# Sliding-window attention and squared-ReLU MLP: Q and K of batches 2 to 7 turned by transposing DMAs instead of 32x32 blocks on VectorE

## The chip, the cores and the metric

The kernel runs on one core of a Trainium2 chip. The metric is the device time of one execution in microseconds, as the median of several runs. TensorE (PE), VectorE (DVE), ScalarE (ACT), GpSimd (POOL) and SyncE (SP) run side by side, each with its own list of instructions, which it takes strictly in order; semaphores tie the lists together. SP and POOL issue DMAs, which 16 DMA engines carry out.

## The reference

```
# q, k, v: [8 batches, 8 heads, 576 tokens, 64], float32
scores = q @ k.T / sqrt(64)                    # within a head
mask   = |i - j| <= 32                         # a window of 65 tokens
attn   = softmax(where(mask, scores, -1e9))
x      = (attn @ v), heads side by side        # [4608 tokens, 512]
h      = x @ w_in                              # [512, 2048]
out    = (max(h, 0) ** 2) @ w_out              # [4608, 512]
```

## The kernel before, in words

**Attention.** A step is 64 queries of one batch with all 8 heads; there are 9 steps a batch, 72 in all. A step's scores (`scores`) are 8 matmuls into one PSUM bank, `sc`: the K tile `KT` (for two heads 128 rows, one half a head, with 32 zero columns at each end) against the zero-padded Q tile `QZ`, in which each head has its 64 rows and zeros in the other 64, so that two heads share one pass. ScalarE takes the exponential, VectorE multiplies by the mask (`pt`), `av` multiplies with V (and a column of ones, which yields the sum), VectorE divides (`rs`, `xr`). The result xr must be turned so that features lie on partitions (`xt`): in the first 26 steps by TensorE and a ScalarE copy, from then on by a transposing DMA issued by SP (`xturn`).

**MLP.** Tokens come in blocks of 512, nine blocks. `mm1` makes 512 columns of h from xt (`ht`), ScalarE the ReLU (`rt`), VectorE the square (`gt`); `mm2` accumulates 128 tokens of output in `outp`, ScalarE copies it to `oe`, SP stores it. Most matmuls are done in two halves of 64 columns (the mode "col" of `matmul`).

**How Q, K and V come in.** POOL issues all loads; they cast float32 to bfloat16. For batches 0 and 1, Q and K come token by token (`fine_load`: pieces of 128 tokens, the last of 64, eight runs of 64 elements a token), TensorE turns each piece (`fine_turn`), VectorE copies K into `KT`, ScalarE copies Q twice into `QZ` with a scale of 1 or 0 for each half, which also writes the zeros. For batches 2 to 7, `load_qk` brings four pairs of heads per tensor, with four tokens side by side (256 elements); `turn` lets VectorE turn 32x32 blocks into the stage `ST`, 16 instructions a batch; `spread` sends the stage to its rows in `KT` and `QZ` by 16 DMAs a batch, issued by SP. Every score of such a batch waits for all 16 (`qk_tags`). V goes to `VD`, and `copy_v` makes a second copy shifted by 64 tokens, `VX`, on VectorE.

**What sets the order.** Every operation is recorded (`Prog.rec`) with what it reads and writes, a planned duration and a key. `schedule` plays the whole program through with these durations and, on each engine, takes the ready operation with the smallest key; that order is then written out and is fixed. Keys count attention steps: step n has the key n - LEAD, block T of the MLP has keys about 8 T + TM, so LEAD says how far attention runs ahead. `FIRST` is the order of the first 39 loads, weights (`a` for w_in, `b` for w_out) among them; `UNITS` the order of block 0's mm1; `KQ` and `KVL` say how early the loads of later batches are issued, FK, FQ, VK0, VK1, VK, KM, MD, TM shift other keys. In gaps of the plan before 36 us the planner puts filler matmuls on zeros (`outp<-zz`), which keep TensorE running.

A transposing DMA as it stands in the kernel before, for xt:

```
e.dma_start(self.XT[:, n % RX].rearrange("p (j h) q -> p j (h q)", j=2), xr[:], transpose=True)
```

Of the kernel before, what the change touches and what calls it, by code (L numbers as in the profile page):

```python
# [31 lines left out]
UNITS = (  # L32
    (0, 128, 0), (128, 128, 4), (256, 256, 2), (128, 128, 12), (0, 128, 12), (128, 128, 8), (0, 128, 8),
    (256, 256, 14), (256, 256, 8), (0, 128, 4), (256, 256, 4), (128, 128, 0), (256, 256, 6), (256, 256, 10),
    (256, 256, 12), (256, 256, 0),
)
FIRST = (
# [6 lines left out]
)  # L44
WCH = ((0, 512), (512, 512), (1024, 1024))
# [213 lines left out]
class Gen:  # L259
# [5 lines left out]
    def alloc(self):  # L265
# [8 lines left out]
        self.RAW = {t: [sb(f"{t}raw{i}", [128, 9, 4, 64], BF16) for i in range(2)] for t in "qk"}  # L274
        self.ST = {t: sb(f"{t}st", [128, 2, 1152], BF16) for t in "qk"}
# [71 lines left out]
    def fine_load(self, b, t, x, key):  # L347
        t0, n = PIECES[x]
        s = (self.q if t == "q" else self.k)[b][:, t0:t0 + n, :].rearrange("h p d -> p h d")
        d = self.FR[t][b][0:n, x, :, :]  # L350
        self.p.rec("POOL", lambda e: e.dma_start(d, s), writes=[("fraw", b, t, x)], dma=(f"f{b}{t}{x}", 0), key=key,  # L351
                   dur=900 if n == 128 else 700, move=(n // 2, 14))

    def fine_turn(self, b, t, x, key):
# [13 lines left out]
        self.p.rec("PE", f, reads=[("fraw", b, t, x), "id"] + [("frz", b, t)] * (n < 128), writes=[tag], key=key, dur=4 * 58 if n == 128 else 4 * 30,  # L368
                   mode="col")
        src = ps[:, 0:4 * n].rearrange("p (j c) -> p j c", j=4)  # L370
        if t == "k":
            dst = self.KT[b][:, :, 32 + t0:32 + t0 + n]
            self.p.rec("DVE", lambda e: e.tensor_copy(dst, src), reads=[tag], writes=[("kf", b, x, 0)], key=key,
                       dur=430 if n == 128 else 300)
            return
# [5 lines left out]

    def load_qk(self, b, t, key):
        src = (self.q if t == "q" else self.k)[b]
        raw = self.RAW[t][b % 2]
        for g in range(4):
            s = src[2 * g:2 * g + 2, :, :].rearrange("h s d -> (h s) d").rearrange(
                "(m r j) d -> r m j d", r=32, j=4)
            self.p.rec("POOL", lambda e, g=g, s=s: e.dma_start(raw[32 * g:32 * g + 32], s),  # L388
                       writes=[("raw", t, b % 2, g)], dma=(f"{t}{b % 2}", b), key=key, dur=610, move=(18, 48))
# [20 lines left out]
    def copy_v(self, b, key, s0, s1):  # L410

        i, n = b % 2, s1 - s0
        rd = [("vd", i, s) for s in range(s0, s1)] + [("vdone", i)]
        for r in (0, 64):
            self.p.rec("DVE", lambda e, r=r: e.tensor_copy(self.VX[i][r:r + 64, s0 + r // 64:s1 + r // 64, :, :],  # L415
                                                           self.VD[i][r:r + 64, s0:s1, :, :]),
                       reads=rd, writes=[("vxc", i, r, s + r // 64) for s in range(s0, s1)], key=key,
                       dur=190 + 140 * n)
# [15 lines left out]
    def turn(self, b, t, dh, m0, n, key, gate):  # L434
        raw, st, i = self.RAW[t][b % 2], self.ST[t], b % 2
        src = bass.AP(raw, 256 * m0 + 32 * dh, [[2304, 128], [256, n], [64, 4], [1, 32]])
        dst = bass.AP(st, 1152 * dh + 128 * m0, [[2304, 128], [128, n], [1, 4], [4, 32]])
        self.p.rec("DVE", lambda e: e.transpose(dst, src),  # L438
                   reads=[("raw", t, i, g) for g in range(4)], writes=[("st", t, dh, m0)], key=key,
                   dur=40 + 320 * n, gate=gate)  # L440

    def spread(self, b, t, dh, key):
        st, i = self.ST[t], b % 2
        rd = [("st", t, dh, m0) for m0 in (0, 3, 5, 7)]
        old = [(t + "f", b - 2, x, hm) for x in range(5) for hm in range(2)] if b < 4 else []
        for s in range(2):
            for hm in range(2):
                r, g = 64 * hm + 32 * dh, 2 * s + hm
                dst = self.KT[i][r:r + 32, 2 * s:2 * s + 2, 32:32 + S_] if t == "k" else \
                    self.QZ[i][r:r + 32, 2 * s:2 * s + 2, hm, :]  # L450
                src = st[32 * g:32 * g + 32, dh, :].rearrange("p (h c) -> p h c", h=2)
                self.p.rec("SP", lambda e, a=dst, c=src: e.dma_start(a, c), reads=rd,  # L452
                           writes=[(t, i, s, r)], old=old, dma=(f"{t}t{i}", b), key=key, dur=600, move=(4, 45))


    def qk_tags(self, b, c):
        i = b % 2
        rows = [64 * dh + 32 * hm for dh in range(2) for hm in range(2)]
        rd = [("ktpad", i, 0), ("ktpad", i, 1)]
        if b < 2:  # L460
            for x in range((64 * c) // 128, min(575, 64 * c + 95) // 128 + 1):
                rd += [("kf", b, x, 0)]
            if c:
                rd += [("kf", b, (64 * c - 32) // 128, 0)]
            return rd + [("qf", b, c // 2, 0), ("qf", b, c // 2, 1)]
        return rd + [(t, i, s, r) for t in "qk" for s in range(2) for r in (0, 32, 64, 96)]

    def scores(self, n):
# [5 lines left out]
        def f(e):  # L474
            for j in range(4):
                for u in range(2):
# [7 lines left out]
                   reads=[("sc", n % 2)], writes=[("e", n % 2)], key=key, dur=560)  # L484
# [8 lines left out]
    def av(self, n):  # L493
# [7 lines left out]
        def f(e):  # L501
            for j in range(4):
                for u in range(2):
                    h = 4 * (j // 2) + j % 2 + 2 * u
                    mm = e.matmul(self.AVP[64 * u:64 * u + 64, VE * j:VE * j + VE], pt[:, 128 * j + 64 * u:128 * j + 64 * u + 64],  # L505
# [41 lines left out]
    def mm1(self, T, t0, n, d0, key, mode="col"):  # L547
# [7 lines left out]
        def f(e):  # L555
            for d in range(nd):
                for ft in range(4):
# [6 lines left out]
                   writes=[("ht", k % 2)], key=key, dur=864 if n > 128 else 900, pos=key, mode=mode)  # L564
        self.p.rec("ACT", lambda e: e.activation(rt[:], ht[:], ACTF.Relu), reads=[("ht", k % 2)],  # L565
                   writes=[("rt", k % 4)], key=key, dur=560)
        rr = rt[:].rearrange("p (d t) -> p d t", d=nd)
        us = range(t0 // 128, (t0 + n) // 128)
# [4 lines left out]
    def mm2(self, T, u, seg, key):  # L573
# [11 lines left out]
        if seg == 3:  # L585
            oe = self.OE[x % 3]
            self.p.rec("ACT", lambda e: e.activation(oe[:], op[:], ACTF.Copy), reads=[("outp", x % 2)],  # L587
                       writes=[("oe", x % 3)], old=[("mtmp", 0), ("mtmp", 1)] if x == 0 else [], key=key, dur=560)
# [109 lines left out]
```

## Time and profile before

| | |
|---|---|
| median of three runs | 319.61 us (317.69 to 320.3) |
| profiled execution | 320.36 us, span 318.7 us, mean granted clock 0.988 |
| busy: PE, DVE, ACT, POOL | 303.1, 211.0, 165.1, 89.0 us |
| DMA queue of POOL (q0) | 73136 packets, 18.36 MB |
| DMA queue of SP (q1) | 26112 packets, 19.54 MB |
| read from and written to HBM | 36.70 and 9.44 MB |

The span is the time from the first to the last instruction in the profiled execution, and its time is a little longer. In the profile, a row of digits is the busy share of 40 equal slices of the span, in tenths; "PE sc L478 <- DMA qz<-qst: 3.6, 3, 2.3" means that TensorE's matmuls at line 478, which write sc, waited for the DMA that writes qz from qst, 3.6 us in total, 3 times, 2.3 at most. Groups list busy time and mean duration in ns of one, then the idle time of the engine just before. SPq and POOLq are the queues of instructions that issue DMAs; "to landing" is the time from the issue to the semaphore that says the data is there.

### The profile page before, as it was taken

Reading aid. Unit: us, or ns where it says so; the run is one execution under the profiler, and the core shown is the slowest. Engines: PE = TensorE matmul, PEld = TensorE weight load, DVE = VectorE, ACT = ScalarE, POOL = GpSimd, SP = SyncE. Lnnn points to the kernel's source line nnn. Section 1 sums busy time; section 2 is a strip of 40 time slices with the busy share of each in tenths; the row PEclk is TensorE's granted clock in tenths of the full one; section 3 lists DMA queues with packets and bytes.
Section 4 is the critical chain, followed back from the end, with each engine's and each line's share of the span. In section 5 each row is a group of like instructions: output and inputs, shape, how many; then the busy total and the mean of one; then the engine's idle time right before and its main releaser. Section 6 shows DMA issues by size and latency. Waiting matters only on the chain.

```text
span 318.7 us, 9690 instructions
## 1 busy us (share of the span) xinstructions
PE 303.1 (95%) x4065; PEld 205.5 (64%) x4065; DVE 211.0 (66%) x529; ACT 165.1 (52%) x303; POOL 89.0 (28%) x128
## 2 busy tenths in 40 slices
PE   6798999998999999979989999999999999999995
PEld 2466887877977776757546666665665666556552
DVE  7475686958798888868848888898744444323300
ACT  2387767545835662446435645643654555435511
POOL 8999992432142324401504211100000000000000
PEclk9799999999999999999979999999999999999999
DMA  9999999999969948993999596635411211210021
GB/s 58 145 186 200 174 189 187 201 229 237 117 105 183 172 49 129 190 215 48 137 176 161 54 161 102 138 79 110 118 50 51 68 43 43 59 69 33 2 100 67
DMA packets 99291, 38.52 MB, mean 121 GB/s; under 512 B 72624, under 2 KB 93616, under 8 KB 99248
## 3 DMA queue, kind: packets, MB, share of 16 engines
q0 software_dynamic: 73136, 18.36, 60.2%
q1 hardware_dynamic: 26112, 19.54, 22.0%
q8 instruction: 32, 0.52, 0.7%
q14 instruction: 11, 0.09, 0.1%
HBM read 36.70 MB, written 9.44 MB: 145 GB/s over the span
## 4 chain that ended last, share of the span: by engine, by line
PE 77%; DMA 12%; POOL 4%; SPq 2%; DVE 2%; ACT 1%; issue 1%; ACTq 0%
PE outp L53 34%; PE ht L53 33%; DMA qz<-qst 5%; PE sc L478 4%; DMA w<-in_moe_w_in_dram 4%; DMA xt<-xr 3%; PE avp L505 2%; PE ht L51 2%; SPq L452 2%; POOL qfr L351 2%; POOL kfr L351 1%; POOL vd L397 1%; ACT rt L565 1%; PE sc L364 1%; PE trp L537 1%
## 5 line engine op out<-in xcount | busy, mean ns | idle before, releaser
L53 PE MATMUL outp<-w,gt 128*64 128x512 bf16 x1152 | 140.6, 379 | 0.0
L53 PE MATMUL ht<-xt,w 128*64 128x512 bf16 (+1 forms) x1280 | 134.6, 351 | 2.8 <-DMA xt<-xr 2.1
L565 ACT ACTIVATE rt<-ht 128x512 bf16<-128x512 f32 x144 | 85.9, 597 | 70.1 <-PE ht L53 57.7
L53 PEld LDWEIGHTS ht<-xt,w 128*64 128x64 bf16 x1280 | 85.0, 137 | 33.6 <-DMA xt<-xr 3.2
L569 DVE TENSOR_TENSOR gt<-rt 128x512 bf16<-128x512 bf16 x144 | 60.5, 422 | 54.3 <-ACT rt L565 52.8
L53 PEld LDWEIGHTS outp<-w,gt 128*64 128x64 bf16 x1152 | 67.4, 110 | 38.7
L483 ACT ACTIVATE e<-sc 128x512 bf16<-128x512 f32 x72 | 42.2, 595 | 20.1 <-PE sc L478 18.6
L397 POOL DMA_DIRECT2D vd<-in_v_dram x32 | 30.1, 972 | 56.0 <-PE avp L505 26.8
L587 ACT ACTIVATE oe<-outp 128x512 f32<-128x512 f32 x36 | 21.5, 598 | 44.2 <-PE outp L53 44.2
L438 DVE STREAM_TRANSPOSE kst<-kraw 128x256 bf16<-128x256 bf16 (+1 forms) x48 | 37.4, 821 | 0.3 <-DMA kraw<-in_k_dram 0.3
L438 DVE STREAM_TRANSPOSE qst<-qraw 128x256 bf16<-128x256 bf16 (+1 forms) x48 | 36.0, 824 | 0.0
L490 DVE TENSOR_TENSOR pt<-e,mask 128x512 bf16<-128x512 bf16 x72 | 29.8, 417 | 6.4 <-ACT e L483 5.4
L519 DVE TENSOR_TENSOR xr<-avp,rs 128x256 bf16<-128x256 f32 x72 | 30.5, 423 | 1.0
L478 PE MATMUL sc<-qz,kt 128*64 128x128 bf16 x576 | 27.0, 221 | 3.7 <-DMA qz<-qst 3.6
L478 PEld LDWEIGHTS sc<-qz,kt 128*64 128x64 bf16 x576 | 22.2, 111 | 12.1 <-issue 4.6
L517 DVE RECIPROCAL rs<-avp 128x4 f32<-128x4 f32 x72 | 13.1, 181 | 20.2 <-PE avp L505 19.6
L388 POOL DMA_DIRECT2D qraw<-in_q_dram x24 | 15.0, 668 | 23.4 <-DVE qst L438 15.8
L405 POOL DMA_DIRECT2D vx<-in_v_dram x16 | 10.2, 639 | 32.2 <-PE avp L505 27.6
L415 DVE COPY vx<-vd 64x528 bf16<-64x528 bf16 (+1 forms) x28 | 16.9, 608 | 3.1 <-DMA vd<-in_v_dram 2.6
L388 POOL DMA_DIRECT2D kraw<-in_k_dram x24 | 14.7, 653 | 7.9 <-DVE kst L438 7.1
L378 ACT ACTIVATE qz<-sc,half 128x512 bf16<-128x512 bf16 (+1 forms) x20 | 12.1, 647 | 9.1 <-PE sc L364 9.0
L505 PEld LDWEIGHTS avp<-vx,pt 128*64 128x64 bf16 x320 | 11.8, 112 | 4.8 <-issue 0.7
(40 smaller groups left out, 144.6 us busy)
## 6 DMA issues: line engine op xcount, KB each, us to landing
out_dram<-oe SPq DMA_DIRECT2D x36, 256.0 KB, 2.4
vd<-in_v_dram POOLq DMA_DIRECT2D x32, 128.0 KB, 5.7
kraw<-in_k_dram POOLq DMA_DIRECT2D x24, 144.0 KB, 11.2
qraw<-in_q_dram POOLq DMA_DIRECT2D x24, 144.0 KB, 10.0
kt<-kst SPq DMA_DIRECT2D x48, 72.0 KB, 3.4
qz<-qst SPq DMA_DIRECT2D x48, 72.0 KB, 3.5
w<-in_moe_w_out_dram POOLq DMA_DIRECT2D x4, 512.0 KB, 17.4
qfr<-in_q_dram POOLq DMA_DIRECT2D x8, 128.0 KB, 4.9
```

Source lines behind the costliest of these rows:

```text
L53: mm = e.matmul(out[r:r + 64], w[:, r:r + 64], x, start=start, stop=stop)
L388: self.p.rec("POOL", lambda e, g=g, s=s: e.dma_start(raw[32 * g:32 * g + 32], s), writes=[("raw", t, b % 2, g)], dma=(f"{t}{b % 2}", b), k ...
L397: self.p.rec("POOL", lambda e, s=s: e.dma_start(self.VD[i][:, s, :, 0:64], v[b, :, 32 + 128 * s:160 + 128 * s, :].rearrange("h p d -> p h ...
L438: self.p.rec("DVE", lambda e: e.transpose(dst, src), reads=[("raw", t, i, g) for g in range(4)], writes=[("st", t, dh, m0)], key=key, dur= ...
L478: mm = e.matmul(sc[64 * u:64 * u + 64, 128 * j:128 * j + 128], self.KT[i][:, j, at:at + 64], self.QZ[i][:, j, :, 64 * c:64 * c + 64], star ...
L483: self.p.rec("ACT", lambda e: e.activation(self.E[n % 2][:], sc[:], ACTF.Exp, scale=0.125), reads=[("sc", n % 2)], writes=[("e", n % 2)], ...
L490: self.p.rec("DVE", lambda e: e.tensor_tensor(pt, ee, mb, ALU.mult), reads=[("e", n % 2), ("mask", mi)], writes=[("pt", n % 2)], key=key, ...
L505: mm = e.matmul(self.AVP[64 * u:64 * u + 64, VE * j:VE * j + VE], pt[:, 128 * j + 64 * u:128 * j + 64 * u + 64], vt[:, h, 0:VE], start=Tru ...
L519: self.p.rec("DVE", lambda e: e.tensor_tensor(bass.AP(xr, 0, [[256, 128], [64, 4], [1, 64]]), bass.AP(self.AVP, 0, [[512, 128], [VE, 4], [ ...
L565: self.p.rec("ACT", lambda e: e.activation(rt[:], ht[:], ACTF.Relu), reads=[("ht", k % 2)], writes=[("rt", k % 4)], key=key, dur=560)
L569: self.p.rec("DVE", lambda e: e.tensor_tensor(gt[:, d0:d0 + nd, t0:t0 + n], rr, rr, ALU.mult), reads=[("rt", k % 4)], writes=[("gt", T % 2 ...
L587: self.p.rec("ACT", lambda e: e.activation(oe[:], op[:], ACTF.Copy), reads=[("outp", x % 2)], writes=[("oe", x % 3)], old=[("mtmp", 0), (" ...
```

## The change

Q and K of batches 2 to 7 now take the same token-wise loads as batches 0 and 1 (`fine_load`, into the same two sets of buffers `FR`). Each piece is then turned by one transposing DMA on SP (`dma_turn`): K straight into `KT`, Q into a new tile `QT`; 10 a batch, 48 of 128 tokens and 12 of 64 in all. VectorE copies `QT` into the two halves of `QZ` (`spread_q`), once for pieces 0 and 1 and once for pieces 2 to 4, so four copies a batch; the zeros in the other halves stay from batches 0 and 1. Heads now lie in their natural order in `QZ` and `KT`, and `fine_turn` and `av` follow. The scores wait only for the pieces that they read (`qk_tags`). The raw buffers, the stage, `turn`, `spread` and `load_qk` are gone. The input weights come in four quarters instead of a quarter, a quarter and a half, and one of them is the first load of all; 32 steps instead of 26 are turned on TensorE; and the constants of the plan, `FIRST` and `UNITS` are others, so that the written order differs throughout. The engines named in VENG and KENG are VectorE, as before. Planned durations of ScalarE's 512-wide operations go from 560 to 600 ns, which touches the order only.

```
-LEAD = 11
+LEAD = 12
-NPE = 26
+NPE = 32
-TOFF, TST, TREL = 5, 0.4, 35
-TOFF2 = 20
-FK, FQ = 14.5, 16.0
-VK0, VK1, VK = 22.0, 1.0, -4.0
-KM, MD, TM = -22.0, 0.5, 3.5
-KQ, KVL = 44, 44
+QCUT = 2
+TK, TQ, TX, TE = 17.0, 36.5, 3.8, 2.0
+FK, FQ = 3.75, 7.75
+VK0, VK1, VK = -2.5, 7.75, -3.0
+KM, MD, TM = 0.5, 0.25, 4.25
+KQ, KVL = 81.0, 28.0
...
-    ("v", 0, 2), ("e", 0, False), ("q", 0, 2), ("k", 0, 1), ("q", 0, 0), ("k", 0, 0), ("q", 0, 1),
+    ("a", 0, 1), ("v", 0, 0), ("q", 0, 0), ("e", 0, False), ("k", 0, 0), ("k", 0, 1), ("k", 0, 2),
...
-WCH = ((0, 512), (512, 512), (1024, 1024))
+WCH = ((0, 512), (512, 512), (1024, 512), (1536, 512))
...
-        self.RAW = {t: [sb(f"{t}raw{i}", [128, 9, 4, 64], BF16) for i in range(2)] for t in "qk"}
-        self.ST = {t: sb(f"{t}st", [128, 2, 1152], BF16) for t in "qk"}
+        self.QT = sb("qt", [128, 4, S_], BF16)
...
+    def dma_turn(self, b, t, x, key):
+        i = b % 2
+        t0, n = PIECES[x]
+        dst = self.KT[i][:, :, 32 + t0:32 + t0 + n] if t == "k" else self.QT[:, :, t0:t0 + n]
+        src = self.FR[t][i][0:n, x, :, :].rearrange("p h d -> p (h d)")
+        self.p.rec("SP", lambda e: e.dma_start(dst, src, transpose=True), reads=[("fraw", i, t, x)],
+                   writes=[("kf", i, x, 0) if t == "k" else ("qt", x)], dma=(f"{t}t{i}{x}", b), key=key, dur=1270,
+                   move=(n // 4, 21))
+
+    def spread_q(self, b, xs, key):
+        i = b % 2
+        t0, t1 = PIECES[xs[0]][0], sum(PIECES[xs[-1]])
+        for hm in range(2):
+            dst, src = self.QZ[i][64 * hm:64 * hm + 64, :, hm, t0:t1], self.QT[64 * hm:64 * hm + 64, :, t0:t1]
+            self.p.rec("DVE", lambda e, d=dst, c=src: e.tensor_copy(d, c), reads=[("qt", x) for x in xs],
+                       writes=[("qf", i, x, hm) for x in xs], key=key, dur=170 + (t1 - t0) * 4 // 4)
...
     # fine_turn
-                    h = 4 * (j // 2) + j % 2 + 2 * u
+                    h = 2 * j + u
...
     # qk_tags
-        return rd + [(t, i, s, r) for t in "qk" for s in range(2) for r in (0, 32, 64, 96)]
+        rd += [("kf", i, x, 0) for x in range(max(0, 64 * c - 32) // 128, min(575, 64 * c + 95) // 128 + 1)]
+        return rd + [("qf", i, c // 2, 0), ("qf", i, c // 2, 1)]
...
     # av
-                    mm = e.matmul(..., pt[:, 128 * j + 64 * u:128 * j + 64 * u + 64], ...)
+                    mm = e.matmul(..., pt[:, 64 * h:64 * h + 64], ...)
...
     # build, batches 2 to 7
-                self.load_qk(b, "k", kb)
-                self.load_qk(b, "q", kb)
+                for x in range(5):
+                    self.fine_load(b, "k", x, kb + 0.5 * x)
+                    self.fine_load(b, "q", x, kb + 0.5 * x)
...
-                for st in range(16):
-                    t, dh, m = ("k", "q")[st // 8], st // 4 % 2, st % 4
-                    self.turn(b, t, dh, ...)
-                    if st % 4 == 3:
-                        self.spread(b, t, dh, 9 * b - LEAD - 9)
+                for x in range(5):
+                    self.dma_turn(b, "k", x, 9 * b - LEAD - TK + TX * x)
+                    self.dma_turn(b, "q", x, 9 * b - LEAD - TQ + TX * x)
+                self.spread_q(b, range(QCUT), 9 * b - LEAD - TE)
+                self.spread_q(b, range(QCUT, 5), 9 * b - LEAD - TE + TX * 3)
```

More of the change, by code (lines that the diff above doesn't have):

```diff
@@ L366, in f @@
             return mm
[L368 removed]
+        self.p.rec("PE", f, reads=[("fraw", b % 2, t, x), "id"] + [("frz", b, t)] * (n < 128), writes=[tag], key=key, dur=4 * 58 if n == 128 else 4 * 30,
                    mode="col")
@@ L372, in fine_turn @@
             dst = self.KT[b][:, :, 32 + t0:32 + t0 + n]
-            self.p.rec("DVE", lambda e: e.tensor_copy(dst, src), reads=[tag], writes=[("kf", b, x, 0)], key=key,
-                       dur=430 if n == 128 else 300)
+            on = KENG[b]
+            self.p.rec(on, lambda e: e.tensor_copy(dst, src) if on == "DVE" else e.activation(dst, src, ACTF.Copy),
+                       reads=[tag], writes=[("kf", b, x, 0)], key=key,
+                       dur=(430 if n == 128 else 430) if on == "DVE" else (600 if n == 128 else 390))
             return
@@ L379, in fine_turn @@
                        reads=[tag, "half"], writes=[("qf", b, x, hm)], key=key, dur=690 if n == 128 else 480)
[L382 to L389, printed above, removed]
     def load_v_at(self, b, s, key):
@@ L483, in scores @@
         self.p.rec("ACT", lambda e: e.activation(self.E[n % 2][:], sc[:], ACTF.Exp, scale=0.125),
-                   reads=[("sc", n % 2)], writes=[("e", n % 2)], key=key, dur=560)
+                   reads=[("sc", n % 2)], writes=[("e", n % 2)], key=key, dur=600)
         mi = 0 if c % 2 else (2 if c == 0 else 3 if c == NCH - 1 else 1)
```

62 lines of the change are left out of this document (18 added, 44 removed), and 10 rows, old and new, of the table FIRST.

## The prediction

> **What bounds the kernel now.** I read the page first, then the table by stage, the waits, the chain, and last the groups and transfers of what the change touches.
>
> ```profile
> span 318.7 us, 9690 instructions
> ...
> PE 303.1 (95%) x4065; PEld 205.5 (64%) x4065; DVE 211.0 (66%) x529; ACT 165.1 (52%) x303; POOL 89.0 (28%) x128
> ...
> PE   6798999998999999979989999999999999999995
> ...
> DMA  9999999999969948993999596635411211210021
> ...
> q0 software_dynamic: 73136, 18.36, 60.2%
> q1 hardware_dynamic: 26112, 19.54, 22.0%
> ```
>
> TensorE is busy in 303.1 of 318.7 us, nearly without a gap from the second slice on. The change leaves its matmuls as they are, but for turns and fillers; so the gain can only come from the holes in the PE row and from the start, and it is small by nature. The DMA row is the other thing to see: full for the first 85 us, which is where the new, smaller loads must fit.
>
> ```profile
> core 0: us, PE busy (x) PEld busy (x) DVE busy (x) ACT busy (x) POOL busy (x), PEclk, DMA share, GB/s
> 140.00:160.00 20.00, 16.81 (x248) 11.96 (x248) 15.50 (x38) 9.68 (x18) 5.65 (x8) 1.00 0.84 117
> 160.00:180.00 20.00, 19.28 (x202) 11.76 (x204) 14.09 (x35) 10.53 (x18) 4.25 (x7) 0.91 0.92 141
> ```
>
> The table by stage puts the largest hole of the middle here: 3.2 us idle in 140 to 160, and a granted clock of 0.91 in the stretch behind it. The waits say for what:
>
> ```profile
> PE sc L478 <- DMA qz<-qst: 3.6, 3, 2.3
> PE ht L53 <- DMA xt<-xr: 2.1, 1, 2.1
> PE ht L51 <- DMA w<-in_moe_w_in_dram: 1.0, 1, 1.0
> ```
>
> The chain shows the two mechanisms behind them:
>
> ```profile
> 137.05 4.62 DMA qz<-qst
> ...
> 142.23 1.73 PE ht L53 x16
> ...
> 153.38 1.24 DVE kst L438 x2
> 154.72 5.95 DMA xt<-xr
> 160.72 3.37 PE ht L53 x16
> ```
>
> Scores of a batch wait for the last of its 16 spread DMAs, since every score of a batch reads all of them. The second wait is an xt turn that came out late, behind two 32x32 turns on VectorE, and then took 5.95 us. The matmuls behind that hole ran at half speed: 3.37 us for what took 1.73 before, 1.6 us more. So the late xt cost 2.1 + 1.6 = 3.7 us.
>
> **The change, part by part.**
>
> *VectorE's 32x32 turns go, copies into the Q tile come.*
>
> ```profile
> L438 DVE STREAM_TRANSPOSE kst<-kraw 128x256 bf16<-128x256 bf16 (+1 forms) x48 | 37.4, 821 | 0.3 <-DMA kraw<-in_k_dram 0.3
> L438 DVE STREAM_TRANSPOSE qst<-qraw 128x256 bf16<-128x256 bf16 (+1 forms) x48 | 36.0, 824 | 0.0
> L415 DVE COPY vx<-vd 64x2112 bf16<-64x2112 bf16 x12 | 8.6, 717 | 0.2
> ```
>
> 73.4 us go. 24 copies come, of 64x1024 and 64x1280. By the 64x2112 copy scaled with its length they take 0.35 and 0.43 us, unscaled 0.72: 9 to 17 us, I take 10. VectorE falls to about 148 us. It bounds nothing by itself; what counts is that no burst of turns stands in front of the products that feed xt.
>
> *96 spreads go, 60 transposing DMAs come, on the same SP queue, in order with xt and the output stores.*
>
> ```profile
> L452 SPq DMA_DIRECT2D kt<-kst x48: 589/598/1519, 57.8 to 217.3; - x48
> L452 SPq DMA_DIRECT2D qz<-qst x48: 586/597/1807, 64.5 to 228.0; - x48
> L529 SPq DMA_TRANSPOSE xt<-xr x46: 1167/1248/2512, 108.3 to 276.6; - x46
> DMA to landing us min/median/max: 2.3/3.0/6.3
> L589 SPq DMA_DIRECT2D out_dram<-oe x36: 332/434/603, 54.0 to 316.2; - x36
> ```
>
> Out: 96 x 0.60 = 58 us of SP. In: 60 turns. The nearest row is xt, 128x256, at 1.25 us; the new turn is 128x512 in 48 cases and 64x512 in 12. Low end 1.25 each, 75 us; high end by size, 48 x 2.5 + 12 x 1.25 = 135 us. Six xt fewer on SP save 7.5. SP holds 131 us now (58 + 46 x 1.25 + 36 x 0.43); after, 140 to 201, in the 222 us between the first store and the last xt. I take the low end, because xt and the new turn are one kind of operation over the same 128 partitions. Then it is hidden by the 80 us that SP has left. What it costs when that cover is gone is the rival below.
>
> *What the scores wait for* becomes piecewise: a score reads the one or two K pieces and the one Q piece that hold its columns, and a turn can start when its own piece has landed, not when four loads of a tensor have. Written out, batch 2's first turns stand behind the first store on SP, and the first score needs two K and Q pieces instead of 16 DMAs. So I take the whole 3.6 us of qz waits off. Bounds: 3.6 gained, or, where kt or qt pieces come late in their turn, the same again lost.
>
> *The late xt.* With the turns off VectorE its product is on time, but SP now has 1.25 us turns ahead of xt where it had 0.60 us spreads. Bounds 0 and 3.7; I take 1.9.
>
> *Loads: 48 raw loads become 60 token-wise pieces.* The same bytes from HBM, written in runs of 128 bytes where raw wrote 512.
>
> ```profile
> 31.47 1.15 POOL L351 DMA_DIRECT2D qfr<-in_q_dram  x1
> ...
> 37.10 0.90 POOL L405 DMA_DIRECT2D vx<-in_v_dram  x1
> ```
> ```profile
> qfr<-in_q_dram POOLq DMA_DIRECT2D x1, 128.0 KB, 21.2
> vx<-in_v_dram POOLq DMA_DIRECT2D x1, 32.0 KB, 22.2
> ```
> ```profile
> GB/s 24 51 91 152 139 84 46 43 29 34 92 130 153 118 88 89 103 120 131 150 152 154 148 150 140 144 127 124 136 133 145 133 144 153 142 145 148 146 155 146
> ```
>
> Eight raw loads stand between the qfr issued at 31.47 (landed 52.7) and the vx at 37.10 (landed 59.3): 6.6 us, 0.83 each of 144 KB. The last row is the stretch from 3 to 13 us, where only token-wise pieces move: about 145 GB/s, 0.90 us for 128 KB. A batch's 576 tokens of Q and K are nine such pieces' worth, 8.1 us against 6.6: 1.5 us more a batch, 3 us for the two batches that fall into the full stretch.
>
> The Trainium skill (DMA: Bandwidth & Descriptors, Specifications) speaks against this: below 512 bytes a transfer is read, modified and written. If that doubled raw's price a byte, a batch would need 13 us, and the sum would be up to 10 us worse for the two batches in the full stretch; the rows just shown do not bear it out.
>
> ```profile
> vd<-in_v_dram POOLq DMA_DIRECT2D x1, 128.0 KB, 27.1
> ```
> ```profile
> vd<-in_v_dram POOLq DMA_DIRECT2D x1, 128.0 KB, 4.4
> ```
>
> A V load issued at 48.1 us took 27.1 to land, one at 84.3 took 4.4: the backlog ends at about 85. What hides the longer loads is the MLP of the first two blocks, which stands ahead of batch 2 on PE. V of batch 2 is now issued behind all of batch 2's Q and K and some of batch 3's, about six microseconds later than now. I charge 1.0 (bounds 0 and 5). On POOL itself
>
> ```profile
> L388 POOL DMA_DIRECT2D kraw<-in_k_dram x24 | 14.7, 653 | 7.9 <-DVE kst L438 7.1
> L351 POOL DMA_DIRECT2D qfr<-in_q_dram x10 | 9.6, 966 | 0.0
> ```
>
> 30 us of raw issues become at most 60 x 0.97 = 58; POOL rises from 89 to some 117 of 318 and is hidden.
>
> *The start.* The second quarter of the input weights is loaded first of all instead of 16th. The first MLP matmul could not start before it landed:
>
> ```profile
> 23.82 1.08 PE L51 MATMUL ht<-xt,w 128*128 128x128 bf16 x16
> ...
> L53 PE MATMUL outp<-zz 128*64 128x512 bf16 x72 | 11.7, 421 | 0.0
> L537 PE MATMUL trp<-ident,xr 128*64 128x128 bf16 x104 | 7.9, 220 | 0.0
> ```
>
> The order now brings five scores instead of seven ahead of that matmul, and writes out 50 half-width fillers instead of 72. 22 x 11.7/72 = 3.6 us of filler fewer. A filler stands where something is waited for, so part comes back as waiting; I take 2.3, and the 1.0 us weight wait. Bounds together 0 and 5. Six more turns of xr on PE (24 matmuls by 7.9/104) are at most 1.8 us; matmuls of a group overlap, so I take 0.7.
>
> **The sum.** 318.7 - 3.6 (qz) - 1.9 (xt) - 2.3 - 1.0 (start) + 0.7 (PE turns) + 1.0 (V of batch 2) = 311.6 us of span. The profiled execution took 320.36, 1.66 more than its span: 313.3. It was 0.75 above the median of the three runs, 319.61: **312.5 us**.
>
> **Rivals.**
>
> *Slower: SP becomes too slow for xt.* If a 128x512 turn holds SP for 2.5 us, SP is held 201 of its 222 us. It is in order: behind a turn that waits for scores or for its piece stand xt and the stores, behind xt stands VectorE's write of xr four steps on, and PE's first matmul of the next block. The written order has five blocks that first wait on PE for xt turns. At the 3.7 us that one such wait cost, hole and slow matmuls, five cost 18.5, where 1.8 remains in my sum: 312.5 + 16.7 = 329 us. It decides from about 2.2 us a turn, where SP is 85% held. For it: twice the elements, and the one late xt of now. Against it: no row shows that SP's time for a turn grows with its size, and xt turns issued close together land no later:
>
> ```profile
> 191.67 3.83 SPq L529 DMA_TRANSPOSE xt<-xr  x3
> ```
> ```profile
> xt<-xr SPq DMA_TRANSPOSE x3, 2.7
> ```
>
> The Trainium skill (VectorE: DVE Perf Modes, The three transpose paths) gives 1309 ns for a 128x128 block by DMA and 311 for the same area on VectorE. If blocks went one after the other, the 216 new blocks would need 283 us and this rival would be certain. The rows here, three xt of two blocks each, issued in 3.83 us and each landed after 2.7, are too close together for that.
>
> *Nothing gained.* The DMA engines are full until 85 us, so an earlier weight chunk only delays Q and K, the filler saved turns into waiting, and V or Q of batch 2 arrives late: the start's 3.3 comes to nothing, V costs 5 instead of 1, and the late xt stays: 312.5 + 3.3 + 4 + 1.9 = 321.7. The full DMA row speaks for it; that the bytes are the same, and that first use in the written order follows the loads, against.
>
> *More gained.* The start gives all 5, no xt is late, V costs nothing: 312.5 - 1.7 - 1.8 - 1.0 = 308, and 306 if the smaller gaps close too. For it: VectorE's load falls by 60 us.
>
> That the change does not do what it says is unlikely: the zero halves of the Q tile are written in batches 0 and 1 and stay.
>
> **How the numbers follow.** My forecast, 309 to 316: 0.52. More gained: 0.14. Nothing gained, 317 to 323: 0.18. SP too slow, 323 to 335: 0.16. A measurement of this kernel tells about 1% from no change: 316.4 and 322.8 are the borders. Faster 0.67, same 0.16, slower 0.17. The range for 8 in 10 reaches from 305.5 to 325.5: the better case and the near half of the worse one.
>
> **What would show it.** Right: no PE wait on qz or kt DMAs over 0.5 us; SP turns of 128x512 near 1.25 us, xt landing still near 3 us; VectorE near 150 us; the first MLP matmul before 21 us; granted clock 1.0 in the 160s. Wrong: turns of 2 us and more on SP, PE waits on xt at several blocks with low clock behind them, VectorE waiting for xt DMAs; V of batch 2 landing after 70 us with a hole behind it; a start that is no earlier because early pieces of Q and K wait behind weights.

## The result, and the profile after

The changed kernel took 333.11 us (median of 4 runs, 330.81 to 334.45) beside 318.97 for the kernel before (317.69 to 320.30): a ratio of 1.0435 [1.0358, 1.0512], slower. The profiled execution took 332.54 with a span of 330.5. The forecast was 312.5, its range 305.5 to 325.5: wrong in sign and outside the range.

The page of the changed kernel, the same parts as shown of before:

```profile
span 330.5 us, 9695 instructions
...
PE 304.6 (92%) x4067; PEld 208.7 (63%) x4068; DVE 160.7 (49%) x457; ACT 167.4 (51%) x309; POOL 111.4 (34%) x141
...
PE   6899999877993999999998958999999999999996
...
DMA  9999999999999999999999966421112112100012
...
q0 software_dynamic: 115328, 18.36, 81.1%
q1 hardware_dynamic: 46272, 19.15, 32.6%
```

TensorE's work is nearly what it was, 304.6 us against 303.1. Its idle time rose from 15.6 us (318.7 - 303.1) to 25.9. The DMA row stands at 9 until about 190 us, where before it first left 9 at about 88. Where the idle time lies is read from the table by stage, first after, then before, in the same stretches (busy time of PE, instructions, granted clock, DMA share, GB/s; this DMA share adds up the times of packets that overlap, so it can exceed 1):

```profile
20.00:60.00 40.00, 39.01 (x706) 1.00 1.80 177
60.00:120.00 60.00, 49.16 (x806) 0.94 1.99 155
120.00:180.00 60.00, 58.32 (x755) 1.00 1.82 155
180.00:220.00 40.00, 35.25 (x414) 0.96 0.63 92
```
```profile
20.00:60.00 40.00, 38.12 (x767) 1.00 1.65 190
60.00:120.00 60.00, 58.61 (x882) 1.00 1.09 161
120.00:180.00 60.00, 55.59 (x676) 0.97 0.96 142
180.00:220.00 40.00, 40.00 (x528) 1.00 0.59 112
```

Idle in 60 to 120 us: 10.8 after, 1.4 before. In 120 to 180: 1.7 after, 4.4 before, so the hole that the forecast wanted closed did close. In 180 to 220: 4.8 after, none before. The two new holes are the result, and they turn out to have different causes. The waits of the changed kernel name what they were for:

```profile
DVE vx L428 <- DMA vd<-in_v_dram: 14.7, 6, 7.4
...
PE trp L521 <- DVE xr L503: 7.8, 3, 5.8
...
DVE qz L369 <- DMA qt<-qfr: 7.0, 2, 5.2
...
DVE xr L503 <- DMA xt<-xr: 5.2, 3, 3.5
```

No wait of PE on a K or Q tile is left. PE waits for VectorE's xr, and VectorE, which works in order, stands before the copies of V. The chain between 75 and 110 us shows it in order of time:

```profile
77.06 24.78 DMA vd<-in_v_dram
101.96 0.70 DVE vx L428
...
104.07 0.35 DVE xr L503
...
105.11 3.41 PE ht L55 x16
```

A V load of batch 3, issued at 77.06, landed 24.8 us later. VectorE's timeline has the two longest waits of its copies, for batch 2 and for batch 3 (start, us, and in brackets the idle time before):

```profile
76.77 0.70 DVE L428 COPY vx<-vd 64x2112 bf16<-64x2112 bf16 x1 [4.68 <-DMA vd<-in_v_dram]
...
101.96 1.44 DVE L428 COPY vx<-vd 64x2112 bf16<-64x2112 bf16 x2 [7.39 <-DMA vd<-in_v_dram]
```

The vx copy, then xr, then PE stood behind the load, and the first matmuls after the hole ran at half speed (3.41 us for what takes 1.75 later). The same stretch, 60 to 80 us, in the transfers of the changed kernel and then of the kernel before (the GB/s row is 40 slices of half a microsecond; the others count, KB and median us to landing):

```profile
GB/s 252 325 178 157 184 150 132 9 37 150 160 150 158 157 155 246 315 196 148 155 181 149 84 9 146 154 157 152 295 308 148 153 151 153 152 155 187 148 41 8
...
vd<-in_v_dram POOLq DMA_DIRECT2D x3, 128.0 KB, 23.3
qt<-qfr SPq DMA_TRANSPOSE x4, 8.1
```
```profile
GB/s 167 175 186 189 215 235 236 243 203 213 253 312 334 239 232 233 222 216 220 213 203 199 166 193 250 322 289 229 243 248 258 194 278 288 201 211 191 195 195 192
```

Both are full, but the engines moved some 150 GB/s after and over 200 before. What POOL's queue of loads got of that, in the same 20 us (packets, MB), after, before, and in e2 below, which leaves nearly all turns out:

```profile
q0 software_dynamic: 11433, 1.44, 125.0%
```
```profile
q0 software_dynamic: 8170, 2.54, 115.7%
```
```profile
q0 software_dynamic: 19149, 2.41, 191.5%
```

The Trainium skill (DMA: Bandwidth & Descriptors, Queues, rings and completion order) says that an engine takes turns between its queues packet by packet. The trace agrees in so far as a turn on SP's queue landed in 8.1 us beside loads that stood 23 us in POOL's: the turns pass the loads, and the loads get 1.44 MB instead of 2.4 to 2.5.

### The profile page after: what moved, and what is told of

Read it like the earlier page. It is cut to its first block, busy times and chain, and to the rows that moved or that the text cites. A ratio compares the mean times of both kernels' runs of the same rounds, so it can differ in the third digit from the quotient of the medians.

```text
span 330.5 us, 9695 instructions
## 1 busy us (share of the span) xinstructions
PE 304.6 (92%) x4067; PEld 208.7 (63%) x4068; DVE 160.7 (49%) x457; ACT 167.4 (51%) x309; POOL 111.4 (34%) x141
## 4 chain that ended last, share of the span: by engine, by line
PE 58%; DMA 21%; POOL 12%; DVE 3%; issue 3%; SPq 2%; ACT 0%; DVEq 0%; POOLq 0%; ACTq 0%
PE ht L55 28%; PE outp L55 25%; DMA vd<-in_v_dram 14%; DMA qt<-qfr 5%; POOL kfr L352 4%; POOL qfr L352 4%; DMA xt<-xr 3%; PE sc L462 3%; POOL vd L408 2%; PE avp L489 2%; SPq L360 1%; DVE vx L428 1%; POOL w L435 1%; DVE gt L553 1%; DVE xr L503 1%
## 5 line engine op out<-in xcount | busy, mean ns | idle before, releaser
L55 PE MATMUL outp<-w,gt 128*64 128x512 bf16 x1152 | 143.5, 381 | 1.0 <-issue 1.0
L55 PE MATMUL ht<-xt,w 128*64 128x512 bf16 (+1 forms) x1280 | 139.0, 355 | 2.6 <-ACT rt L550 1.6
L55 PEld LDWEIGHTS ht<-xt,w 128*64 128x64 bf16 x1280 | 86.1, 138 | 31.4 <-issue 4.7
L55 PEld LDWEIGHTS outp<-w,gt 128*64 128x64 bf16 x1152 | 69.5, 110 | 39.6 <-issue 2.2
L408 POOL DMA_DIRECT2D vd<-in_v_dram x32 | 29.3, 919 | 70.0 <-PE avp L489 44.9
L352 POOL DMA_DIRECT2D kfr<-in_k_dram x40 | 34.9, 897 | 12.2 <-issue 4.1
L352 POOL DMA_DIRECT2D qfr<-in_q_dram x40 | 36.0, 908 | 2.8 <-PE sc L462 1.9
L428 DVE COPY vx<-vd 64x528 bf16<-64x528 bf16 (+1 forms) x28 | 16.4, 586 | 15.2 <-DMA vd<-in_v_dram 14.7
L526 ACT ACTIVATE xt<-trp 128x256 bf16<-128x256 bf16 x32 | 12.2, 383 | 12.7 <-PE trp L521 12.4
L521 PE MATMUL trp<-ident,xr 128*64 128x128 bf16 x128 | 9.7, 225 | 8.2 <-DVE xr L503 7.8
L369 DVE COPY qz<-qt 64x1024 bf16<-64x1024 bf16 (+1 forms) x24 | 12.7, 530 | 8.2 <-DMA qt<-qfr 7.0
```

Of the source, the lines that this page charges most:

```text
L55: mm = e.matmul(out[r:r + 64], w[:, r:r + 64], x, start=start, stop=stop)
L408: self.p.rec("POOL", lambda e, s=s: e.dma_start(self.VD[i][:, s, :, 0:64], v[b, :, 32 + 128 * s:160 + 128 * s, :].rearrange("h p d -> p h ...
L428: self.p.rec(on, lambda e, d=dst, c=src: e.tensor_copy(d, c) if on == "DVE" else e.activation(d, c, ACTF.Copy), reads=rd, writes=[("vxc", ...
```

## The experiments

The questions, by the letters that the expectations use: A, the many small packets of the token loads fill the DMA engines; B, the order on POOL's queue, V's place in it; C, SP is too slow; D, a turn occupies the DMA engines longer than a copy. In the form of the prediction's rival, 2.5 us a turn, C fell by the first profile: SP held a 128x512 turn no longer than xt.

```profile
L360 SPq DMA_TRANSPOSE kt<-kfr x30: 1190/1234/2477, 48.5 to 214.1; - x30
L360 SPq DMA_TRANSPOSE qt<-qfr x30: 1171/1268/2277, 49.9 to 187.1; - x30
```

That says nothing yet of the stretches in which many turns come together; see the late hole below.

**Larger runs, and turns left out.**

```
e1  s = k[b] as one flat stretch, (p c) -> p c with c=512   # 128 packets a load, not 1024
e2  turn = t == "q" and b == 2;  all others copy 16x32 B    # 55 of 60 turns gone
e3  both
e4  the kernel before: raw loads "(m j r) d" for "(m r j) d" # 1152 packets a load, not 288
```

> The changed kernel with its written order and all its waits as they are; the 60 Q and K loads of batches 2 to 7 move the same bytes, but in runs of 512 elements instead of 64 (128 packets a load instead of 1024), so Q and K hold other values. Theory A (the DMA engines are full because of the number of packets, V lands late behind them, VectorE's copies of V wait): 48 thousand packets of 162 thousand go, the full stretch ends near 110 us instead of 180, V waits under 3 us, time 312 to 320. Theory B (the order is at fault, V is simply issued too late): V still waits over 10 us, 328 to 334. Theory C (SP is too slow with its turns): 328 to 334.

> The changed kernel with its written order and all its waits; 55 of the 60 transposing DMAs (all but Q of batch 2) are replaced by copies of 16 rows of 32 bytes, so K and Q of batches 2 to 7 are not turned. Theory A: some 28 thousand packets go, the full stretch ends near 140 us, time 316 to 324. If the turns take the DMA engines more than by their packets, it comes down to 310 to 316. Theory B: over 328. Theory C (SP): the copies take SP 0.6 instead of 1.25 us; if SP was the bound, 312 to 318, and xt waits fall.

> Both cuts at once: Q and K loads in runs of 512 elements and 55 of 60 turns replaced by small copies (Q and K wrong and not turned), order and waits as in the changed kernel. Theory A: the DMA engines are free from about 90 us, no wait for V, 307 to 313, which is what the order is worth without the transfers' cost. Theory B: over 325.

> The kernel before, its written order unchanged; its 48 raw loads move the same bytes in runs of 64 elements instead of 256 (1152 packets a load instead of 288), so tokens are permuted. Theory A: 41 thousand packets more, the full stretch of 85 us grows to 110 or more, Q, K or V of batches 2 to 4 late, 322 to 330. Theory B (only the changed order matters): 318 to 320.

Measured: e1 333.67 us, ratio to before 1.0484 [1.0403, 1.0565]; e2 313.81, 0.9865 [0.9805, 0.9926]; e3 312.91, 0.9828 [0.9757, 0.9898]; e4 1.0005 [0.9958, 1.0051]. An eighth of the packets helped nothing, and four times the packets cost the kernel before nothing: A is out. Without its turns the changed kernel is below the kernel before, by 1.4 and 1.7%, with intervals that do not reach 1: all of its loss hangs on them. The page of e2 and its wait on V:

```profile
PE   8889999987889999999999999999999999999996
...
DMA  9999999999999998999955583311111111100021
```
```profile
DVE vx L431 <- DMA vd<-in_v_dram: 1.5, 3, 0.7
```

**Order and kind.**

```
e5  KQ, KVL = 81.0, 60.0      e6  KQ, KVL = 44.0, 44.0      # keys of K, Q and of V
e7  128x512 turns: e.dma_start(dst, src.rearrange("p (j c) -> p j c", j=4))  # 48 plain copies
```

> The changed kernel with V of batches 2 to 7 due 32 steps earlier (KVL 60 instead of 28); the planner writes the order anew. Theory D: the DMA engines are as full as before; V comes earlier but Q and K later, 325 to 335. Theory B (only V's place is at fault): 312 to 320, no wait for V.

> The changed kernel with Q and K due when the kernel before had them, and V too (KQ and KVL 44); planned anew. Theory D: 324 to 336, the wait moves from V to the turned Q and K. Theory B: 312 to 320.

> The changed kernel with its order and waits; the 48 turns of 128 tokens are plain copies of the same 128 KB from the piece to the same tile, 512 runs of 256 bytes, so Q and K are not turned; the 12 turns of 64 tokens stay. Theory D (a turn takes the DMA engines far longer than a copy of the same bytes and packets): 312 to 319, V waits under 4 us. Theory A' (it is the bytes and packets between SBUF and SBUF on the queue that SP shares, whatever their kind): 326 to 334, V waits over 10 us.

Measured: e5 331.96, 1.0337 [1.0258, 1.0416]; e6 334.85, 1.0471 [1.0393, 1.0548]; e7 322.14, 1.0072 [1.0034, 1.0111]. New keys changed little. e5 was a poor test: V of batch 2 still went out behind the same loads of K and Q, since its key remained behind theirs and its buffer is read by batch 0 until then. e7, between the times that its two theories gave, says that moving the bytes costs part and transposing them more: from e2 to e7 2.1%, from e7, in which 12 turns of 64 tokens are left, to the changed kernel 3.6%.

**The transfers by themselves.** e8 issues 16 of each kind alone; e9 issues 24 token loads on POOL's queue four times: alone, beside 24 turns, beside 24 plain copies of 128 KB, beside 42 spreads of 72 KB.

> Transfers by themselves, nothing computed, the output is zeros: one after the other 16 turns of 128x512, 16 of 128x256, 16 spreads of 72 KB, 16 token-wise loads, 16 loads in runs of 256 elements, 16 in runs of 512. Theory D: a turn of 128x512 keeps the 16 engines busy 0.9 us or more (over 100 us times engines in all for a batch of 10), a spread under 0.3. Theory A': a turn under 0.5 us of all engines, by its 544 packets; token-wise loads near 0.9 us, the others 0.7 to 0.85.

> Not the kernel: four stretches, each with 24 token loads of 128 KB on POOL's queue (1024 runs of 128 B each): alone; beside 24 transposing DMAs 128x512 on SP; beside 24 plain copies of the same 128 KB inside the on-chip memory (512 runs of 256 B); beside 42 spread copies of 72 KB. From the pieces measured alone (a load 0.9 us of all engines, a turn 0.64, a spread 0.30) the four stretches would take 21.6, 37.0, about 37 and 34.2 us if the DMA engines do the two kinds one after the other without loss (capacity theory: turns and spreads alike, so the changed kernel's crowding must come from elsewhere, the order of the loads). If transposing and loading hamper each other (theory of the mix), the second stretch takes clearly longer than 37 us, 45 or more, the third and fourth do not.

In e8 SP issued 16 turns in 20.94 us, 1.31 each, and each landed after 2.5 us; by the share of busy engines a turn took 0.64 us of all of them. That was not far from what a spread costs per byte, and it lies between what D (0.9) and its rival (0.5) had asked for. Only the mix tells them apart. The timeline of e9, POOL and SP:

```profile
2.59 13.25 POOL L30 DMA_DIRECT2D tok<-in_q_dram  x15 [2.15 <-DVEq L21]
...
31.34 13.13 POOL L30 DMA_DIRECT2D tok<-in_q_dram  x15 [3.83 <-DMA tok<-in_q_dram]
...
74.50 13.11 POOL L30 DMA_DIRECT2D tok<-in_q_dram  x15 [7.42 <-DMA tok<-in_q_dram]
...
112.72 13.12 POOL L30 DMA_DIRECT2D tok<-in_q_dram  x15 [3.52 <-DMA tok<-in_q_dram]
```
```profile
147.54 23.74 SPq L55 DMA_DIRECT2D out_dram<-z  x36
```

Each stretch ends where the next begins: 28.75 us alone, 43.16 with turns, 38.22 with copies, 34.8 with spreads. So a turn added 0.60 us, a copy 0.39, and a spread 0.145 (0.26 for 128 KB). These are differences in length. The stretch alone has POOL's pause of 3.8 us in it, in which the queue ran empty, so its 1.2 us a load are too many and the prices of what came beside the loads rather too few. Where the queues were full, the loads alone moved 140 GB/s (5 to 15 us). A full part of the stretch with turns (34 to 60 us), and of that with spreads (115 to 138 us), by queue, POOL's loads first:

```profile
q0 software_dynamic: 15318, 1.93, 119.7%
q1 hardware_dynamic: 9286, 2.23, 65.1%
```
```profile
q0 software_dynamic: 16426, 2.07, 141.1%
q1 hardware_dynamic: 1687, 2.60, 36.7%
```

With turns that is 74 GB/s of loads and 86 of turns, 160 together; with spreads 90 and 113, 203 together. The bytes of a turn displace the bytes of a load nearly one for one, those of a spread only about half: the rest comes on top. These are close to the rates of the two kernels at 60 to 80 us. The size of the runs does not make that difference: e4, with the changed kernel's runs of 128 bytes beside spreads, moved 206 GB/s in that stretch, and e1, with larger runs beside turns, 154.

**V first, and the new start alone.**

```
g2  K and Q loads of batch b > 2:  op.order |= set(v_ops)   # V loads of batch b-1
h1  the kernel before with FIRST, UNITS, WCH, LEAD, NPE and the keys of the changed one, but KQ, KVL = 44, 44
```

> The changed kernel with one constraint for its planner: in POOL's list the K and Q loads of batch b (3 to 7) stand behind the V loads of batch b-1. The same transfers, no new wait at run time. If V is late because the K and Q loads of later batches, issued early, stand ahead of it in the queue (crowding), V's waits on VectorE fall from 14.7 us to below 5 and the time to 312 to 320 us. If the DMA engines simply have too much to do until 180 us whatever the order (capacity or the mix), K or Q is late instead of V, and the time stays at 328 to 335 us.

> The kernel before with its raw loads, 32x32 turns and spreads of batches 2 to 7 kept, and with the changed kernel's start alone: its order of first loads, its UNITS, W1 in four quarters, LEAD 12, NPE 32, its keys. If the changed kernel's early lead (work that stood at 24.2 us before stands at 19.6 us) is worth keeping where no turn on the DMA engines takes it back, 313 to 317 us; if the lead is lost again in the second half of the program whatever feeds it (PE waits on something else there), 318 to 320 us, as before.

Measured: g2 337.25, 1.0533 [1.0427, 1.0639]; h1 322.97, 1.0138 [1.0054, 1.0223]. V went ahead and was still waited for (18.7 us on VectorE), because V of a batch can be asked for only after attention two batches earlier has read its buffer; K and Q now waited for that too. h1 missed both of its expectations. Its first MLP matmul starts at 19.10 us as in the changed kernel, but it has 8.3 us of idle PE in 60 to 120 us, where the kernel before has 1.4. The longest wait behind that is one that the changed kernel cannot have. PE waits 6.0 us, until 64.8, for VectorE's copy of a K piece of batch 1, and VectorE, in order, has all 16 of batch 2's 32x32 turns ahead of it:

```profile
54.07 5.34 DVE L438 STREAM_TRANSPOSE kst<-kraw 128x384 bf16<-128x384 bf16 x8
59.23 5.28 DVE L438 STREAM_TRANSPOSE qst<-qraw 128x384 bf16<-128x384 bf16 x8
64.32 0.43 DVE L373 COPY kt<-sc 128x512 bf16<-128x512 bf16 x1
```

So h1 says that the start gains nothing where these turns stay in this written order; it does not say that the start alone is worth nothing.

**Where the turns cost, and a third buffer for V.**

```
k1  VD and VX: range(3), i = b % 3;  KVL = 82.0
k2  turn = not (b == 3 or (b == 2 and t == "k"))    # 15 of 60 turns gone
k3  turn = not (b > 5 or (b == 5 and t == "k"))     # 25 of 60 turns gone
```

> The changed kernel with three buffers for V (VD and VX) in place of two, and V's key moved so that V of batch b is asked for together with K and Q of batch b. All transfers and turns stay. If the loss is V's place in the queue (it can be asked for only when attention of batch b-2 has read its buffer, and then stands 25 us behind), VectorE's wait on V (14.7 us) goes below 3 us and the time to 314 to 321 us. If the DMA engines are simply full until 180 us, Q or K is late in V's place and the time stays above 327 us.

> The changed kernel with 15 of its 60 turns left out: K of batch 2, Q and K of batch 3 (16x32 B copies in their place, so this output is not the reference's). If the turns cost only while the backlog of 45 to 110 us lasts (a), these 15 bring back most of the 20 us: 315 to 321 us. If each turn costs a third of a microsecond wherever it is (b), they bring 5 us: 328 us.

> The changed kernel with 25 of its 60 turns left out, late ones: K of batch 5, Q and K of batches 6 and 7 (16x32 B copies in their place, so this output is not the reference's). By (a) they bring little: 329 to 333 us. By (b) 25 turns bring 8 us: 325 us.

Measured: k1 334.57, 1.0495 [1.0413, 1.0577]; k2 322.83, 1.0119 [1.0074, 1.0164]; k3 324.43, 1.0170 [1.0092, 1.0248]. With a third buffer V is asked for earlier, and what is asked for between 60 and 80 us still takes 23.2 us to land. So V comes earlier, batch 3's last piece at 85.0 us instead of 101.8, batch 5's at 125.7 instead of 145.8. But the new plan also set VectorE's copies of V earlier in its order, and they waited as long as before:

```profile
DVE vx L428 <- DMA vd<-in_v_dram: 17.6, 7, 5.1
```

So V's place in the queue is not by itself what costs the time. k2 fell between (a) and (b), nearer to (a); k3 came out as (b) said. Against the changed kernel 15 early turns are worth 3.2%, 10 us, 0.67 each, and 25 late ones 2.7%, 8.5 us, 0.34 each. Both kinds cost, an early one twice as much as a late one.

**Other traffic taken away, and early turns on TensorE.**

```
k4  dma_start(out[128 * x:128 * x + r, :], oe[0:r, :]),  r = 8 if x < 18 else 128
k5  if b < 4: fine_turn(...)   # for b < 2;  dma_turn and spread_q only for b > 3
```

> The changed kernel with the first 18 of its 36 output stores cut to 8 of 128 rows (16 KB for 256 KB; the output is not the reference's); every turn, load and the order on every engine stay. 13 of these stores fall before 182 us in the changed kernel; a store alone took 0.66 us of all DMA engines, so 8.6 us of their work go. If the loss is the DMA engines' capacity whoever uses it, the six stores before 110 us (4 us of work) bring what turns brought there per us of work (10.3 us for 15 turns of 0.60), 4.6 us, and the seven later ones (4.6 us) 2.7: about 326 us. If only transposing DMAs hamper the loads, the time stays at 331 to 334 us.

> The changed kernel with Q and K of batches 2 and 3 turned on TensorE as those of batches 0 and 1 are; 40 turning DMAs of batches 4 to 7 stay. A turn on TensorE costs 8 matmuls, about 0.22 us of its time, 20 of them 4.4 us, and 60 more copies on ScalarE and VectorE, which are half idle. Leaving 15 of these out brought 10.3 us, so 20 would bring some 13: 333.1 - 13 + 4.4 = about 324.5 us if the copies hide, 328 to 331 us if ScalarE's longer Q copies (0.64 us each) delay its exponentials and TensorE's score banks.

Measured: k4 326.68, 1.0234 [1.0145, 1.0323]; k5 325.88, 1.0181 [1.0118, 1.0244]. In k4 every turn and every load is where it was, and 8.6 us less of other DMA work brought 2.0%, 6.4 us, as the theory of capacity had said (326). Where V is late it is the engines' time that is short, whoever uses it. VectorE's wait on V fell from 14.7 us to 8.6 in k4 and to 8.2 in k5.

k5 keeps the whole computation and is the best form of the change that was run, but it does not beat the kernel before. Since even without its turns the change gains only 1.4 to 1.7% (e2, e3), and a turn costs something wherever it was put, no version that beats both was in sight, and none was run.

**What the runs say together.** The early hole, 60 to 120 us, comes of the DMA engines' time. An estimate of a batch's share of it, by the lengths in e9: 13.5 loads of 128 KB (nine of Q and K, four and two quarters of V) at 28.75 / 24 = 1.2 us are 16.2; eight turns of 0.60 and two of half the size 5.4; some 2.4 output stores at 0.66 (36 alone took 23.74 us) 1.6. That is 23.2 us with turns, 16.2 + 16 x 0.145 + 1.6 = 20.1 with spreads, 17.8 with neither; xt's turns are not counted. The sums are too high by the pause in the stretch alone (at 140 GB/s a load takes 0.94 us), so only their differences are used here. At 45 us all versions have loads queued that take 15 to 23 us to land. How fast that queue drains is seen directly: a V load issued at 80 to 100 us still took 23 us (median) with turns, and 4 to 5 with spreads (the kernel before) or with neither (e2, e3). Twelve sets of turns at 2.7 us make 32.4, 96 spreads 13.9: 18.5 us more engine time. For each microsecond of it taken away the runs got back 0.6 (e2), 0.75 (k4), 1.15 (e7: 48 x 0.21) and 1.25 (k2). For k3 the same division gives 0.6, but its turns cost in another way as well.

The late hole, 180 to 220 us, is not simply the same shortage again. VectorE did wait for a turn of Q that took 6.8 us to land:

```profile
177.65 0.48 DVE L369 COPY qz<-qt 64x1280 bf16<-64x1280 bf16 x1 [5.18 <-DMA qt<-qfr]
```

But PE's waits of the hole come later, where the DMA share is 0.63 and no longer 1.8, and they hang on xt:

```profile
196.66 2.38 DMA xt<-xr
...
199.18 3.28 PE ht L55 x16
```

What was full here was SP. From 130 to 200 us it spent 94% of its time issuing (78% before), and each xt turn stood in order behind turns of Q and K. One xr and the SP queue behind it:

```profile
183.65 0.42 DVE L503 TENSOR_TENSOR xr<-avp,rs 128x256 bf16<-128x256 f32 x1
```
```profile
183.43 4.87 SPq L360 DMA_TRANSPOSE qt<-qfr  x3
188.35 1.24 SPq L513 DMA_TRANSPOSE xt<-xr  x1
189.68 1.22 SPq L360 DMA_TRANSPOSE kt<-kfr  x1
190.95 1.24 SPq L513 DMA_TRANSPOSE xt<-xr  x1
```

The turn of the xr that was done at 184.07 is the one issued at 190.95, 6.9 us later; the one at 188.35 belongs to the step before. Over the steps whose xr was written between 150 and 205 us this delay was 6.4 us on average, beside 1.5 in the kernel before; the time from issue to landing was about the same (4.5 and 3.7). VectorE's write of xr four steps on waits for it, then PE, and the matmuls behind the hole ran at half speed again. In e2 and k3, without the late turns, the delay was 0.3 and 0.4 us and PE had no wait in 180 to 220 us; in k2, with only early turns left out, it was 5.2 us and a hole of 3.5 us remained. No run leaves the turns on the engines and takes them off SP alone, so how much of k3's 8.5 us is SP's is not shown.

Open: why e1 gained nothing. With 128 packets a load its stretches between 60 and 100 us moved 154 and 168 GB/s, against 159 and 151 in the changed kernel, with more half-microseconds at 8 or 9 GB/s; its turns landed after about 10 us instead of 8. Its late hole is no puzzle, since xt stood 7.1 us on SP there too. That loads which are cheaper alone are not cheaper beside turns was seen, not explained.

## Why the prediction was wrong, point by point

- *The turns, priced on SP and "hidden by the 80 us that SP has left".* This is the step that failed, in two ways. A DMA occupies the queue that issues it and also the engines that carry it, and only the first was counted. The second is 0.60 us a turn where a spread is 0.145: 18.5 us more, in a stretch whose DMA row the prediction itself had called full. That made the early hole. And the 80 us that SP had left were an average over 222 us: the price of a turn on SP was right (1.23 and 1.27 us, 1.25 taken), but from 130 to 200 us SP was issuing 94% of the time, and xt stood behind the turns. That is seen in the late hole. "The backlog ends at about 85" was read from the kernel before and taken over; with the turns' share a V load issued at 105.8 us still took 12.5 to land. The rows to price the engines from were thin, since the kernel before has only xt turns, in stretches with few loads. But the plan in the two kernels books such a price: `move=(n // 4, 21)` is 32 x 21 = 672 ns of the shared engines for a turn of 128 tokens, `move=(4, 45)` 180 ns for a spread. Added up over all of them that is 19 us more, and the prediction did not add it up.
- *V of batch 2, 1.0 us, bounds 0 to 5.* The mechanism was named and listed under what would prove the forecast wrong, V landing after 70 us with a hole behind it; that is what came, VectorE waiting until 76.8 us for batch 2 and until 102.0 for batch 3. The size was off: 9.4 us more idle time in 60 to 120 us, and slow matmuls behind it. V of batch 2 was asked for 9 to 11 us later than before (46.7 to 51.0 us beside 37.7 to 40.4), not six, and the upper bound thought of one batch; the queue behind which V stood lasted for two.
- *Loads.* "1.5 us more a batch" was harmless: e1, e3 and e4 show that the size of the runs decides nothing in these kernels. The Trainium skill (DMA: Bandwidth & Descriptors, Specifications) has transfers below 512 bytes read, modified and written. No kernel here shows a price for it: e4, with runs of 128 bytes in the kernel before, ran at 1.0005 of its time. Alone, in e8, 16 loads took 20.9 us in runs of 128 bytes, 4.0 of them a pause of POOL, beside 15.2 in runs of 512.
- *What the scores wait for, 3.6 us gained.* Right: no PE wait on a K or Q tile is left, and 120 to 180 us lost 1.7 us of idle time instead of 4.4, at a clock of 1.00. Part came back as VectorE's 7.0 us wait on qt.
- *The late xt, 1.9 of 3.7 gained.* Not realised: xt was late again near 199 us, now by SP's queue, with a matmul group of 3.28 us behind it. The prediction had named the reason, "1.25 us turns ahead of xt where it had 0.60 us spreads".
- *The start, 3.3 us gained.* The first MLP matmul came at 19.11 us instead of 23.82, before the 21 that the prediction named. The same start in the kernel before (h1) gained nothing: there VectorE's 32x32 turns stand in its way.
- *VectorE, 148 us.* It fell to 160.7. The copies took 12.7 us, within 9 to 17, but the groups overlap in time, so taking 73.4 us of turns out freed less than that. VectorE's total bounds nothing here.
- *Six turns on PE, 0.7.* trp rose from 7.9 to 9.7 us: 1.8, the upper bound.
- *The sum without the turns.* 311.6 of span was forecast; e2, which has all of the change but 55 turns, had 311.5. The terms other than the turns add up, but in part by luck: trp took 1.8 where 0.7 was put down, and no run measures the other terms one by one.
- *Rivals.* "SP becomes too slow" gave 329, near the result. Its size is luck, since a turn did not hold SP for 2.5 us and xt did not stop PE at five blocks; but its mechanism, xt in order behind turns, then VectorE's write of xr, then PE, is that of the late hole, 4.8 us of idle time. "Nothing gained" had the mechanism of the early hole, DMA engines full and V late, and let it cost 4 us because "the bytes are the same". They are; the time of the engines was not. The Trainium skill's figure that argued hardest against the change (VectorE: DVE Perf Modes, The three transpose paths, 1309 ns for a block of 128x128 by DMA) is not borne out as a price to be added up block by block. By it a 128x512 turn of four such blocks would take 5.2 us (an estimate); it held SP for 1.25 us and added 0.60 us to a full queue.

## What to carry to other kernels

A DMA has two prices, on the queue that issues it and on the shared engines that carry it; where the DMA row is at 9, the second can be the one on the path, even for a transfer nobody waits for. Before moving work from an idle engine to DMA, add up a stage's transfers in engine time and compare with the stage's length: what is left is what drains the queue, and the transfer that can be asked for last (here V, whose buffer is read until late) pays. Do the same for the issuing queue: SP had 80 us left over the whole program and almost none between 130 and 200 us. Then measure the new transfer beside the traffic it will meet, since alone a turn looked nearly as cheap, byte for byte, as a spread.

## What the hardware showed that was not expected

- A mix of token loads and turns moved about 155 to 160 GB/s, little more than loads alone (140 to 150); with plain copies or spreads beside the same loads it was 200 to 220.
- A turn that lands after 2.5 us alone took 7 to 10 us beside loads, and still passed loads that had been queued 23 us.
- POOL issued 15 token loads of 1024 packets one after the other and then paused, 3.8 us alone and 14.7 beside turns, before it issued the next; 16 loads of fewer packets showed no such pause in e8.
- A third buffer and an earlier request made V land up to 20 us earlier, but no sooner after the request, and the kernel no faster.
